# Two constants of RMSNorm in one tile, and the tiles behind them 32 bytes lower in SBUF

## The chip, the cores and the metric

The kernel runs on one core of a Trainium2 chip. The metric is the device time of one execution in microseconds (us); lower is better. Three runs of the kernel before were timed, and one further execution was profiled.

## What is computed

The reference chains three blocks on 3072 tokens of width 512:

```
# 1. chunked attention: 4 x 8 heads, 768 positions, head width 64; chunks of 32 queries see
#    16 positions to the left, 8 to the right, and 8 memory slots
a = exp(s - max(s)); a = a / (sum(a) + 1e-9); x = a @ v          # s = q k^T / 8
# 2. first MoE block, d_ff 1536
xn = x / sqrt(mean(x * x) + 1e-6) * rms_g
y = (silu(xn @ w_gate) * (xn @ w_val)) @ w_out
# 3. second MoE block, d_ff 2048
h = y @ w_in
g = where(h >= 1, h, where(h <= -1, 0, (h + 1)**2 / 4))
out = g @ w_out2
```

## The kernel before

**Stages.** Tokens are handled in 6 tiles of 512 (`TT`). The opening (0 to 36 us of the profile) runs the attention of the first 256-token pairs by an order written out by hand (`ORDER`): `s` is the scores, `m` and `e` their softmax, `a` and `A` a transpose, `v` the product with the values, `n`, `q`, `k` and `p` the normalization, `x` and `X` a transpose of the result. Then the first MoE block takes four of the six tiles one by one (36 to 496 us); the rest of the attention, the conversion of the weights from 64-bit words, and the making of weight sums for later stages run in the slots between its matmuls (`slot`, `att_slot`, `conv_w`, `conv_step`). The last two tiles of the first MoE block go together as a pair (496 to 690 us), and then the second MoE block runs in three pairs of tiles, both with seven products in place of eight.

**Matmuls.** Each product of two float32 matrices is made of three matmuls on a high and a low part (`mm3`, lines 546 to 548; lines 854 to 856 and 990 to 992 in the later stages). In the first MoE block the weights are the stationary operand, from the tile `wall`, and the streamed operand is `xh`, `xl` (the normalized input) or `hh`, `hl` (the hidden values), tiles of 512 float32 columns, 2048 bytes a partition.

**The constants.** `rms_g` is loaded twice by SP, once spread over all partitions as rows (`g_b`, line 629), and once as 4 columns, one for each block of 128 features (`g_t`, line 630). `nhalf` is two columns of -0.5, set by VectorE at the start (line 589). `part_p` (line 498) raises the mean square to the power -0.5 on GpSimd with `nhalf` as the exponent, twelve times, once a pair. From the third pair on `part_X` (line 535) scales by the columns of `g_t` on ScalarE; the first two pairs are multiplied by `g_b` (lines 509 and 651).

**Memory.** Tiles are taken from pools, in the order of the code, each a multiple of 32 bytes a partition. On the left side lie `const` (`half`), `wpool` (`wall`, 147456 bytes), and then the pools of the first MoE block: `const1` with `ident` (512 bytes), `g_b` (2048), `nhalf` (8) and `g_t` (16), then `small`, `wst`, `tmp`, `xs`, `hp`, `sp` and `sums`. The pool `att` of the attention lies on the right side, up to the end of the memory; its tiles `k0`, `k1`, `q`, the rows, `aT` and `e` are 2048 bytes, the two `v` buffers 2080. The last of the left pools ends where `att` begins. When the single tiles are done, `p1` takes the place of `xs` and what follows it; when the first MoE block is done, the pool `m2` begins where `ident` was.

```python
    ident = const1.tile([P, P], F32, name="ident")
    g_b = const1.tile([P, DM], F32, name="g_b")
    nhalf = const1.tile([P, 2], F32, name="nhalf")
    g_t = const1.tile([P, KK], F32, name="g_t")
```

**What sets the order.** In the opening the order on every engine is that of the code. In the first of the four tiles (to about 150 us) the order on TensorE and SP is that of the code, and a planner orders the other engines by its own costs. After that every engine follows the code again. Waits between engines and for transfers are derived from which tiles an instruction reads and writes.

Of the kernel before, what the change touches and what calls it, by code (L numbers as in the profile page):

```python
# [8 lines left out]
F32 = mybir.dt.float32  # L9
# [7 lines left out]
P = 128  # L17
# [21 lines left out]
def tile_stream_attention_moe_moe2(  # L39
# [14 lines left out]
    KK = DM // P  # L54
# [15 lines left out]
    const1 = pool1("const1", 1)  # L70
# [13 lines left out]
    wall = wpool.tile([P, 36, 2, 512], F32R, name="wall")  # L84
    ident = const1.tile([P, P], F32, name="ident")
    g_b = const1.tile([P, DM], F32, name="g_b")
    nhalf = const1.tile([P, 2], F32, name="nhalf")
    g_t = const1.tile([P, KK], F32, name="g_t")


    busy = sums_.tile([P, TT], F32, tag="s34", name="busy").bitcast(BF16)[:, :FILL]
# [1048 lines left out]
```

## Time and profile before

| | us |
|---|---|
| median of 3 runs | 1179.17 |
| lowest and highest run | 1174.78, 1180.15 |
| span of the profiled execution, first to last instruction | 1172.9 |
| matmuls busy in that span | 1151.0 |
| VectorE, ScalarE, GpSimd busy | 741.2, 517.6, 108.0 |

The profiled execution's own time is known by its span. The timed runs also hold what lies before the first and after the last instruction. Busy times are those of the profile; matmuls overlap, so that their durations don't add up to time.

### The profile page before, as it was taken

What the parts mean: (1) busy time and instruction counts of PE and PEld (TensorE: products, weight loads), DVE (VectorE), ACT (ScalarE), POOL (GpSimd) and SP (SyncE); (2) the same over time, 40 slices, a digit from 0 to 9 for tenths busy, and PEclk for the clock granted to TensorE, in tenths of its full rate; (3) what the DMA queues carried; (4) which work ended last, traced back from release to release, by engine and by line L of the source; (5) the groups of instructions that cost most, each with busy time, mean ns of one, the idle gap of its engine ahead of it and who ended that gap; (6) DMA issues with size and microseconds to landing.
All of it is one profiled execution on the core that took longest, in us unless ns stands there. A gap on an engine that the chain in (4) does not pass through costs nothing.

```text
span 1172.9 us, 19949 instructions
## 1 busy us (share of the span) xinstructions
PE 1151.0 (98%) x7993; PEld 936.4 (80%) x7993; DVE 741.2 (63%) x1280; ACT 517.6 (44%) x910; POOL 108.0 (9%) x175
## 2 busy tenths in 40 slices
PE   6899999999999999999999999999999999999998
PEld 4677878887778778878888888888888888888887
DVE  5888865566465655877677576665376662576620
ACT  4766756556665664433333343333143341343310
POOL 2200012212122122201111000000000000000000
PEclk9899999999999999999999999999999999999999
DMA  8566467788767666598898775757466576555364
GB/s 307 177 221 208 153 223 275 282 290 294 276 206 239 223 199 225 199 383 311 305 361 309 283 279 189 261 187 267 158 222 260 195 259 203 191 190 197 135 202 157
DMA packets 98589, 278.60 MB, mean 238 GB/s; under 512 B 10560, under 2 KB 22848, under 8 KB 92096
## 3 DMA queue, kind: packets, MB, share of 16 engines
q1 hardware_dynamic: 79936, 218.59, 52.5%
q0 software_dynamic: 15104, 52.44, 12.3%
q10 hardware_dynamic: 3456, 6.29, 1.4%
q8 instruction: 63, 1.03, 0.3%
q14 instruction: 30, 0.25, 0.1%
HBM read 209.13 MB, written 68.16 MB: 236 GB/s over the span
## 4 chain that ended last, share of the span: by engine, by line
PE 86%; DMA 6%; DVE 4%; ACT 2%; issue 1%; POOL 0%; SPq 0%; ACTq 0%; DVEq 0%; POOLq 0%
PE ps_y L991 7%; PE ps_y L992 7%; PE ps_y L990 7%; PE ps_g L546 6%; PE ps_g L547 6%; PE ps_g L548 6%; PE ps_b L855 5%; PE ps_b L854 5%; PE ps_b L856 5%; PE ps_y L546 5%; PE ps_y L547 5%; PE ps_y L548 5%; PE ps_g L854 4%; PE ps_g L855 4%; PE ps_g L856 4%; DMA w<-in_w_dram 3%
## 5 line engine op out<-in xcount | busy, mean ns | idle before, releaser
L546 PE MATMUL ps_g<-xh,wall 128*128 128x512 f32 x384 | 156.3, 407 | 0.0
L547 PE MATMUL ps_g<-xl,wall 128*128 128x512 f32 x384 | 150.9, 393 | 0.0
L548 PE MATMUL ps_g<-xh,wall 128*128 128x512 f32 x384 | 150.4, 392 | 0.0
L914 ACT ACTIVATE t<-t,half 128x512 f32<-128x512 f32 x96 | 69.0, 720 | 131.2 <-DVE t L913 131.2
L991 PE MATMUL ps_y<-wo,wall 128*128 128x512 f32 x324 | 126.0, 389 | 0.0
L990 PE MATMUL ps_y<-wo,wall 128*128 128x512 f32 x324 | 126.0, 389 | 0.0
L992 PE MATMUL ps_y<-wo,wall 128*128 128x512 f32 x324 | 126.0, 389 | 0.0
L854 PE MATMUL ps_b<-wall 128*128 128x512 f32 x288 | 112.0, 389 | 0.0
L855 PE MATMUL ps_b<-wall 128*128 128x512 f32 x288 | 112.0, 389 | 0.0
L856 PE MATMUL ps_b<-wall 128*128 128x512 f32 x288 | 112.0, 389 | 0.0
L928 DVE TENSOR_TENSOR t<-t,ps_g 128x512 f32<-128x512 f32 x24 | 16.5, 688 | 113.5 <-PE ps_g L856 107.9
L548 PEld LDWEIGHTS ps_g<-xh,wall 128*128 128x128 f32 x384 | 72.6, 189 | 16.1
L854 PE MATMUL ps_g<-wall 128*128 128x512 f32 x216 | 84.2, 390 | 1.1 <-DMA wall<-w1p_d 1.0
L546 PEld LDWEIGHTS ps_g<-xh,wall 128*128 128x128 f32 x384 | 72.6, 189 | 15.8
L855 PE MATMUL ps_g<-wall 128*128 128x512 f32 x216 | 84.1, 389 | 0.0
L856 PE MATMUL ps_g<-wall 128*128 128x512 f32 x216 | 84.0, 389 | 0.0
L547 PEld LDWEIGHTS ps_g<-xl,wall 128*128 128x128 f32 x384 | 72.8, 190 | 13.5
L546 PE MATMUL ps_y<-hh,wall 128*128 128x512 f32 x192 | 77.6, 404 | 0.0
L547 PE MATMUL ps_y<-hl,wall 128*128 128x512 f32 x192 | 75.2, 392 | 0.1
L548 PE MATMUL ps_y<-hh,wall 128*128 128x512 f32 x192 | 74.9, 390 | 0.0
L990 PEld LDWEIGHTS ps_y<-wo,wall 128*128 128x128 f32 x324 | 60.8, 188 | 12.7
L991 PEld LDWEIGHTS ps_y<-wo,wall 128*128 128x128 f32 x324 | 60.8, 188 | 12.6
(157 smaller groups left out, 2240.4 us busy)
## 6 DMA issues: line engine op xcount, KB each, us to landing
wo<-w2o_d SPq DMA_DIRECT2D x100, 512.0 KB, 4.8
wall<-w2p_d SPq DMA_DIRECT2D x24, 1792.0 KB, 7.3
wall<-w1p_d SPq DMA_DIRECT2D x12, 1792.0 KB, 8.6
w<-in_w_dram SPq DMA_DIRECT2D x36, 512.0 KB, 3.9
w<-in_w_dram POOLq DMA_DIRECT2D x32, 512.0 KB, 5.5
k_in<-in_k_dram SPq DMA_DIRECT2D x48, 256.0 KB, 4.6
wo<-w1o_d SPq DMA_DIRECT2D x24, 512.0 KB, 7.9
v_in<-in_v_dram SPq DMA_DIRECT2D x40, 260.0 KB, 4.3
```

Of the source, the lines that this page charges most:

```text
L546: nc.tensor.matmul(ps, wh, xh, start=start, stop=False)
L547: nc.tensor.matmul(ps, wh, xl, start=False, stop=False)
L548: nc.tensor.matmul(ps, wl, xh, start=False, stop=stop)
L854: nc.tensor.matmul(bank, wh, xh, start=st, stop=False, skip_group_check=True)
L855: nc.tensor.matmul(bank, wh, xl, start=False, stop=False, skip_group_check=True)
L856: nc.tensor.matmul(bank, wl, xh, start=False, stop=kk == 1, skip_group_check=True)
L914: nc.scalar.activation(s, s, AF.Square, scale=0.5, bias=half)
L928: tt(out=u2, in0=a, in1=b2, op=ALU.add)
L990: nc.tensor.matmul(ps_y[m], hi[:, sl], wh, start=b == 0, stop=False)
L991: nc.tensor.matmul(ps_y[m], hi[:, sl], wl, start=False, stop=False)
L992: nc.tensor.matmul(ps_y[m], lo[:, sl], wh, start=False, stop=b == F2 - 1)
```

## The change

The tiles `nhalf` and `g_t` become one tile `facts` of 6 columns. Its first 4 columns take the place of `g_t`, the last 2 that of `nhalf`. The names stay, as views of the tile. The code that writes and reads them is unchanged.

```diff
     ident = const1.tile([P, P], F32, name="ident")
     g_b = const1.tile([P, DM], F32, name="g_b")
-    nhalf = const1.tile([P, 2], F32, name="nhalf")
-    g_t = const1.tile([P, KK], F32, name="g_t")
+    facts = const1.tile([P, KK + 2], F32, name="facts")
+    g_t, nhalf = facts[:, :KK], facts[:, KK:]
```

The tiles of the left pools behind `const1` begin 32 bytes lower in each partition: those of `small`, `wst`, `tmp`, `xs`, `hp`, `sp` and `sums`, and later those of `p1`. `wall`, `ident`, `g_b`, the pool `att` and the pool `m2` stay where they are.

## Rows read from the trace of the kernel before

**Rows 1.** The page's first part: busy us (share of the span) and instructions by engine

```profile
PE 1151.0 (98%) x7993; PEld 936.4 (80%) x7993; DVE 741.2 (63%) x1280; ACT 517.6 (44%) x910; POOL 108.0 (9%) x175
```

**Rows 2.** Busy time by stretch: from:to, length, engines, granted clock, DMA share, GB/s

```profile
0.00:36.00 36.00, 23.70 (x651) 16.11 (x652) 21.45 (x45) 17.26 (x41) 13.01 (x18) 0.91 0.88 301
36.00:496.00 460.00, 455.70 (x4387) 365.81 (x4386) 315.73 (x596) 278.36 (x522) 71.04 (x117) 0.99 0.66 229
690.00:1172.90 482.90, 478.88 (x2113) 396.18 (x2111) 269.96 (x431) 153.89 (x236) 0.00 (x0) 1.00 0.58 208
...
36.00:100.00 64.00, 61.34 (x444) 49.05 (x442) 58.30 (x108) 44.85 (x85) 3.89 (x4) 0.94 0.55 188
```

**Rows 3.** Groups of instructions by line: count, busy us, mean ns, idle before

```profile
L546 PE MATMUL ps_g<-xh,wall 128*128 128x512 f32 x384 | 156.3, 407 | 0.0
...
L546 PE MATMUL ps_y<-hh,wall 128*128 128x512 f32 x192 | 77.6, 404 | 0.0
```

**Rows 4.** Timeline of TensorE in the first MoE block: start, duration, instruction

```profile
470.24 0.39 PE L546 MATMUL ps_g<-xh,wall 128*128 128x512 f32 x1
...
471.60 0.39 PE L546 MATMUL ps_g<-xh,wall 128*128 128x512 f32 x1
```

**Rows 5.** Timeline of TensorE in the paired tiles

```profile
559.62 0.39 PE L854 MATMUL ps_b<-wall 128*128 128x512 f32 x1
...
560.98 0.39 PE L854 MATMUL ps_b<-wall 128*128 128x512 f32 x1
```

**Rows 6.** Timeline of the opening, what touches the constants and follows them

```profile
1.20 0.06 DVE L589 MEMSET nhalf<- 128x2 f32 x1
...
14.28 0.43 SPq L630 DMA_DIRECT2D g_t<-in_rms_g_dram  x1
...
20.51 3.16 POOL L651 TENSOR_TENSOR x_nat<-x_nat,g_b 128x256 f32<-128x256 f32 x4 [19.20 <-ACT sq L479]
...
23.64 1.16 POOL L498 TENSOR_TENSOR rs<-ss,nhalf 128x2 f32<-128x2 f32 x1
...
24.83 0.72 ACT L655 ACTIVATE x_nat<-x_nat,rs 128x512 f32<-128x512 f32 x1 [0.64 <-POOL rs L498]
...
25.61 0.66 PE L519 MATMUL ps_s<-ident,x_nat 128*128 128x128 f32 x4 [0.70 <-ACT x_nat L655]
```

**Rows 7.** The tile g_t: its load, and from issue to landing

```profile
L630 SPq DMA_DIRECT2D g_t<-in_rms_g_dram x1: 433/433/433, 14.3 to 14.3; - x1
...
DMA to landing us min/median/max: 5.5/5.5/5.5
```

**Rows 8.** The tiles v_in, then k_in: from issue to landing

```profile
DMA to landing us min/median/max: 2.6/4.4/7.5
...
DMA to landing us min/median/max: 2.7/4.6/8.7
```

**Rows 9.** Lines 463 and 498: duration ns min/median/max, first and last start

```profile
L463 DVE RECIPROCAL rd<-rd x24: 195/203/206, 16.6 to 436.1; 128x8 f32<-128x8 f32 x24
...
L498 POOLq EVENT_SEMAPHORE x1: 17/17/17, 77.2 to 77.2; - x1
```

**Rows 10.** Lines 439 and 393, matmuls of the attention, the same columns

```profile
L439 PE MATMUL ps_a<-v_in,aT x1392: 213/217/263, 16.0 to 435.7; 64*32 64x65 f32 x199
...
L393 PE MATMUL ps_a<-k_in,q_in x1344: 212/216/241, 5.8 to 422.3; 64*32 64x64 f32 x192
```

**Rows 11.** Waits of TensorE: us in total, times, longest us

```profile
PE ps_a L393 <- DMA q_in<-in_q_dram: 2.0, 2, 1.5
...
PE ps_s L393 <- DMA q_in<-in_q_dram: 1.2, 1, 1.2
PE ps_g L854 <- DMA wall<-w1p_d: 1.0, 1, 1.0
```

**Rows 12.** Timeline of the opening: matmuls that fill time

```profile
14.96 1.07 PE L95 MATMUL ps_a<-busy 128*128 128x352 bf16 x6
...
8.62 0.77 PE L95 MATMUL ps_s<-busy 128*128 128x352 bf16 x4
```

## The prediction

> **What bounds the kernel now.** I read the page's totals first, then busy time by stretch, then the groups of instructions, then the waits, and last the few instructions that touch the two constants.
>
> The totals put TensorE at 1151.0 of 1172.9 us [rows 1]: whatever the change does must reach TensorE to count. By stretch [rows 2], the opening 36 us hold 23.70 us of matmuls, the first MoE with attention beside it (36 to 496 us) 455.70 of 460, the last stretch shown 478.88 of 482.90. Outside the opening there are 4.3 + 4.0 us of idle TensorE in those two stretches, and the only wide place is 36 to 100 us (61.34 of 64), where VectorE is busy for 58.30 of 64 us with the conversion of the weights. The matmuls that read a moved tile as their streamed operand are the three lines 546 to 548 with xh, xl, hh or hl [rows 3]: 3 x (384 + 192) = 1728 of them. Their duration is a pipelined latency; what one costs is the distance from start to start. In 470.24 to 471.60 us six pass, 1.36 / 6 = 0.227 us each [rows 4]. In 559.62 to 560.98 us, with operands in the weights' tile, which doesn't move, six pass in the same 1.36 us [rows 5].
>
> The profiled execution has a span of 1172.9 us; the runs have a median of 1179.17, 6.3 us more, which I take as what lies around the span and leave as it is.
>
> **The change, part by part.** *What is added or removed as work: nothing.* The memset of two columns, the 2 KB load, the twelve powers and the scalings are the same instructions. The sum therefore has only waits and addresses in it.
>
> *The shared tile.* If order is kept by tile and not by column, two waits are new. First, the load on SP waits for the memset: that ran at 1.20 us, the load is issued at 14.28 us [rows 6], slack 13 us, cost 0. Behind it on SP stand the loads of v and of the weights; they keep their place. Second, the first power (L498, GpSimd) waits for the load. It lands 5.5 us after its issue [rows 7], at 19.8 us, and the power starts at 23.64 us because GpSimd is in its four multiplications by g_b from 20.51 us on [rows 6]: slack 3.9 us, cost 0. Were that cover gone, the scaling on ScalarE at 24.83 us and then the transposes at 25.61 us would be late by as much, 1 us for 1 us. Of the 48 loads of k the slowest took 8.7 us [rows 8]; with that the constants would land at 22.98 us, still before 23.64. A wait written as an instruction of its own takes 17 ns [rows 9]; only the two powers of the opening have TensorE behind them, so 0.03 us. I take 0.0. The later readers of the constants come after this load by tens of us; all of them are covered.
>
> *The 32 bytes.* Tiles take multiples of 32 bytes: 8 and 16 bytes took two such steps, 24 bytes take one. The pools start on a multiple of 64; `half` takes 32, so the weights, `ident` and `g_b` begin 32 past a multiple of 64, and today everything behind `g_t` does too, since all other tiles there are multiples of 64, or come in pairs of 32. After the change those tiles begin on a multiple of 64, while the weights stay at 32 past. The pool of the second MoE starts where `ident` did and doesn't move; the boundaries of the two pools never coincide (they differ by half of 512 bytes), so a shift of 32 makes no later tile lie over another earlier one, and the waits for reuse stay as they are. What is left is whether an access at 64n + 32 costs other than one at 64n. The trace has three controls, because a few tiles of before lie at both.
>
> VectorE: `rd` has two buffers 32 bytes apart, one at each position. All 24 reciprocals take 195 to 206 ns [rows 9]. The bound is that spread, 11 ns. Where VectorE nearly fills the time (36 to 100 us) it has 108 instructions [rows 2]: 108 x 11 ns = 1.2 us to either side. Elsewhere TensorE has work queued; 0 there. I take 0.
>
> TensorE: a chunk of v is 65 columns, 260 bytes, so successive chunks begin at every multiple of 4 bytes within a 64-byte line; chunks of k are 256 bytes and begin all at one position. The medians are 217 and 216 ns, the least 213 and 212 [rows 10], and the one column more accounts for that. I take 0; as a bound, 1 ns on each of 1728 matmuls is 1.7 us to either side. This control has 64 columns and a float32 stream rather than 512 columns, so it is near, not the same.
>
> Transfers: of the two v buffers of the attention pool one is 2080 bytes behind the other, so at 64n, the other at 64n + 32; all k buffers are at 64n + 32. The medians to landing are 4.4 us for 260 KB and 4.6 us for 256 KB [rows 8]. I take 0; the bound is 0.2 us a transfer. TensorE itself waits for a transfer in four places shown [rows 11], 4.2 us in all: 4 x 0.2 = 0.8 us to either side.
>
> The sum: 1172.9 + 0.0 in the profile, 1179.2 in runs, bounds 1.2 + 1.7 + 0.8 = 3.7 us to either side. For order I add the 4.3 us of idle TensorE in 36 to 496 us: there ScalarE, VectorE and GpSimd are ordered by a planner that sees one tile where it saw two; the most a changed order is likely to do is to lose or give back something of that size. That makes 1171 to 1187 at the outside.
>
> *A rule against the row.* The trace's distance of 227 ns for 512 columns is longer than its own bfloat16 filling matmuls suggest: six take 1.07 us and four 0.77 [rows 12], so 0.15 us for 352 columns, and 218 ns for 512. Nine ns of each large matmul are unexplained by columns. The Trainium skill ("TensorE: Matmul & The Clock Gate", Back-to-back issue gap) gives N/2.4 + 2.5 ns for a matmul at the full clock, 215.8 ns here, so by it too about 11 ns are extra; by that page 1728 x 11 = 19 us would be to be won if the place of the rows were the reason. The Trainium skill ("SBUF — State Buffer", Specifications) puts SBUF's lines at 16 bytes; by that a shift of 32 changes nothing in how a row falls on lines, the extra has another cause, and the sum stays at 0. The controls above agree with the second.
>
> **The rivals.**
>
> *TensorE gets faster.* A row of 2048 bytes at 64n + 32 touches one line of 64 more than a row at 64n; if that is the 9 ns, 1728 x 9 = 15.6 us go: 1164. For it: the extra is there, and every large matmul of before streams from 64n + 32. Against it: the filling matmuls also stream from 64n + 32 and show no extra, and the chunks of v show none. Chance 0.07.
>
> *TensorE gets slower.* After the change the streamed row is at 64n and the weights are at 64n + 32; today both have the same place. If weight load and stream get in each other's way when out of step, and a matmul pays as much again as it does now, 9 ns, the time is 1179.2 + 15.6 = 1195. It decides from 5.9 us / 1728 = 3.4 ns a matmul on. For it: the weight load overlaps the stream in every matmul. Against it: the chunks of v meet their weights at all positions, with 217 ns as median. Chance 0.05.
>
> *The shared tile stalls the opening.* The power waits for a late load. It needs a landing 23.64 - 14.28 = 9.4 us after the issue to cost anything and 9.4 + 5.9 = 15.3 us to cost 0.5%; the slowest load in [rows 8] took 8.7. It stays inside the forecast.
>
> *The change moves nothing* (the space is rounded otherwise, or a planner lays tiles out anew): then the time is 1179 too, and only the addresses would tell.
>
> **How the numbers follow.** A measurement of this kernel can tell about 0.5%, 5.9 us, from no change; its three runs lie 5.4 us apart. No change holds 0.76: the sum is 0 and its bounds of 3.7 us are inside. Faster 0.13: the first rival 0.07, and 0.06 for gains at their bounds together with a better order of the planner. Slower 0.11: the second rival 0.05, and 0.06 for the bounds on the other side, order included. The forecast is 1179 us, the range 1171.5 to 1186.5: the sum with its bounds and the term for the order. It leaves out both rivals on TensorE, 0.12, and a little beyond the bounds.
>
> **What would show it.** In the profile after: the start-to-start distance of lines 546 to 548 stays 0.227 us (a rival if 0.218 or 0.236); reciprocals at 195 to 206 ns and v loads at 4.4 us; the first power starts at about 23.6 us with GpSimd busy before it, and no wait for g_t's load in front of it; TensorE busy for about 455.7 us between 36 and 496. I would be wrong if that distance moved by more than 3.4 ns, if the idle TensorE time of 36 to 100 us doubled, or if an order of instructions on VectorE or ScalarE came out different and cost a wait for weights.

## The result: slower by 0.7%

The changed kernel takes 1185.49 us (median of 4 runs, 1183.39 to 1187.11), the kernel before 1176.97 us on the same chips (4 runs, 1173.36 to 1180.15). The ratio is 1.0072 with an interval of 1.0055 to 1.009: some 8.5 us are lost, outside noise. The forecast was no change, 1171.5 to 1186.5 us; the time lies just inside that range, but the change is real and the forecast was wrong. That it lies inside is luck: the terms that made the range wide (reciprocals, transfers, order) showed no effect, and the kernel before came out 2.2 us below the 1179.17 us that the forecast started from; 1179.17 + 8.5 would lie outside.

The page's totals after, the same line as in [rows 1]:

```profile
PE 1159.8 (98%) x7993; PEld 936.1 (79%) x7993; DVE 741.2 (63%) x1280; ACT 518.1 (44%) x910; POOL 107.8 (9%) x175
```

VectorE, ScalarE and GpSimd are where they were, with the same counts of instructions. TensorE is busy 8.8 us longer with the same 7993 matmuls, and its share stays at 98%: a stream of matmuls that have become slower looks as full as before. The shared tile is innocent in the profile. In the timeline of the opening after (start, duration, engine, instruction) the load is issued at 14.39 us, and the first power follows the four multiplications at once, as in [rows 6]:

```profile
14.39 0.43 SPq L630 DMA_DIRECT2D facts<-in_rms_g_dram  x1
...
20.66 3.17 POOL L651 TENSOR_TENSOR x_nat<-x_nat,g_b 128x256 f32<-128x256 f32 x4 [19.35 <-ACT sq L479]
...
23.79 1.16 POOL L498 TENSOR_TENSOR rs<-ss,facts 128x2 f32<-128x2 f32 x1
```

The controls on VectorE and on transfers stand too: reciprocals still take 203 ns, and the loads of v land after 4.2 us (4.4 in [rows 8]). What moved is the matmul. The timeline of TensorE after, in the same stretch as [rows 4]:

```profile
469.61 0.40 PE L547 MATMUL ps_g<-xl,wall 128*128 128x512 f32 x1
...
471.94 0.40 PE L548 MATMUL ps_y<-hh,wall 128*128 128x512 f32 x1
```

Ten matmuls pass between these two starts, 2.33 / 10 = 0.233 us each, where it was 0.227. The duration shows it as well. Line 547 by its three uses, the inputs and outputs of the single tiles and the outputs of the paired tiles (duration ns min/median/max, first and last start). Before:

```profile
L547 PE MATMUL ps_g<-xl,wall x384: 387/389/628, 39.3 to 490.9; 128*128 128x512 f32 x192
L547 PE MATMUL ps_y<-hl,wall x192: 387/389/497, 51.4 to 496.7; 128*128 128x512 f32 x192
...
L547 PE MATMUL ps_y<-wall,wo x96: 389/389/496, 516.4 to 678.3; 128*128 128x512 f32 x96
```

After:

```profile
L547 PE MATMUL ps_g<-xl,wall x384: 390/396/404, 38.8 to 495.5; 128*128 128x512 f32 x192
L547 PE MATMUL ps_y<-hl,wall x192: 389/396/461, 51.0 to 501.2; 128*128 128x512 f32 x192
...
L547 PE MATMUL ps_y<-wall,wo x96: 392/396/498, 520.9 to 688.3; 128*128 128x512 f32 x96
```

The third row is the surprise: these are the outputs of the paired tiles. Their streamed row lies in `wall`, which did not move. Their weights (`wo`, in the pool `p1`) did. And the products of the later stages, and the outputs of the second MoE block, keep their 389 ns (lines 854 and 990 after):

```profile
L854 PE MATMUL ps_b<-wall x288: 388/389/398, 504.4 to 1123.7; 128*128 128x512 f32 x144
...
L990 PE MATMUL ps_y<-wo,wall x324: 388/389/398, 708.2 to 1167.2; 128*128 128x512 f32 x162
```

So exactly those matmuls became slower of whose two operands one moved and the other stayed. Taken over all neighbouring starts less than 300 ns apart in the two traces, the mean distance (start to start) goes from 228.5 to 233.2 ns in the first MoE block (1561 and 1571 pairs) and from 226.9 to 233.2 in the paired outputs (284 and 282 pairs); the other stages stay at 226.7. With 1728 and 288 matmuls that is 1728 x 4.7 + 288 x 6.3 = 9.9 us, against 8.5 measured.

### The profile page after: what moved, and what is told of

Read it like the earlier page. It is cut to its first block, busy times and chain, and to the rows that moved or that the text cites. A ratio compares the mean times of both kernels' runs of the same rounds, so it can differ in the third digit from the quotient of the medians.

```text
span 1183.0 us, 19949 instructions
## 1 busy us (share of the span) xinstructions
PE 1159.8 (98%) x7993; PEld 936.1 (79%) x7993; DVE 741.2 (63%) x1280; ACT 518.1 (44%) x910; POOL 107.8 (9%) x175
## 4 chain that ended last, share of the span: by engine, by line
PE 89%; DMA 5%; DVE 3%; ACT 2%; issue 1%; SPq 0%; POOL 0%; ACTq 0%; DVEq 0%; POOLq 0%
PE ps_y L992 7%; PE ps_y L991 7%; PE ps_y L990 7%; PE ps_g L546 7%; PE ps_g L548 6%; PE ps_g L547 6%; PE ps_b L856 5%; PE ps_b L854 5%; PE ps_b L855 5%; PE ps_y L546 5%; PE ps_y L547 5%; PE ps_y L548 5%; PE ps_g L854 4%; PE ps_g L856 4%; PE ps_g L855 4%; DMA w<-in_w_dram 2%
```

## The experiments

Three theories were put on record. *Step*: a large matmul costs more when its streamed row and its weights lie at different places; operands at equal places, counted modulo a period that the experiments had to find, are called in step below. *Place*: a row or weights at a multiple of 64 bytes cost more by themselves. *Wait*: sharing the tile adds a wait or changes an order.

**Shared tile, old places** (`e1_gap`).

```diff
     facts = const1.tile([P, KK + 2], F32, name="facts")
+    gap = const1.tile([P, 2], F32, name="gap")
...
+    nc.vector.memset(gap, 0.5)
```

> The changed kernel with an unused tile of 8 bytes behind the shared one (and one memset of it), so that every later tile lies where it lay before. Theory step (a large matmul costs more when its streamed row and its weights lie at different places within 64 bytes): the distance of lines 546 to 548 is back at 0.227 us and the time at that of before, 1177 us. Theory place (a row at a multiple of 64 costs more by itself): the same, 1177. Theory wait (sharing the tile adds a wait or changes the planner's order): it stays near 1185 us.

Measured: 1178.6 us, ratio 1.0002 (0.9992 to 1.0013). In the trace the distance is 228.4 ns in the first MoE block and 226.9 in the paired outputs, those of before. Sharing the tile costs nothing; *wait* falls, and the whole loss is in the 32 bytes. The line that is 547 in the other kernels (`e1_gap`):

```profile
L548 PE MATMUL ps_g<-xl,wall x384: 387/389/402, 40.7 to 491.7; 128*128 128x512 f32 x192
```

**Everything at a multiple of 64** (`e2_all0`).

```diff
-    half = const.tile([P, 1], F32, name="half")
...
     wall = wpool.tile([P, 36, 2, 512], F32R, name="wall")
+    hold = wpool.tile([P, 16], F32, name="hold")
+    half, g_t, nhalf = hold[:, :1], hold[:, 1:KK + 1], hold[:, KK + 1:KK + 3]
...
-    nhalf = const1.tile([P, 2], F32, name="nhalf")
-    g_t = const1.tile([P, KK], F32, name="g_t")
```

> Weights and all other left tiles begin at a multiple of 64 bytes (half, g_t and nhalf share a tile of 64 bytes behind the weights). Streamed rows and weights are in step again, but at 64n, not at 64n + 32. Theory step: 0.227 us everywhere, 1177 us. Theory place: all 4680 large matmuls cost some 6 ns more than before, 0.233 us in every stage, about 1204 us. Should the period be 128 bytes instead of 64, the second MoE block alone shows 0.233 us where weights or rows come from its own pool, which lies 64 bytes out of step here.

Measured: 1180.48 us, ratio 1.0015 (1.0006 to 1.0025). The first MoE block is at 228.3 ns, as before. *Place* falls: 1204 us was its forecast. The small loss that is left sits in the second MoE block, whose pool lies 64 bytes off here. The three lines of its outputs, where rows come from that pool and weights from `wall` (`e2_all0`, lines one up from the original):

```profile
L989 PE MATMUL ps_y<-wo,wall x324: 392/394/398, 700.1 to 1162.7; 128*128 128x512 f32 x162
...
L990 PE MATMUL ps_y<-wo,wall x324: 388/388/397, 700.3 to 1162.9; 128*128 128x512 f32 x162
...
L991 PE MATMUL ps_y<-wo,wall x324: 388/392/398, 700.6 to 1163.1; 128*128 128x512 f32 x162
```

Their mean distance is 229.3 ns: 64 bytes cost something, but less than 32. So the period isn't 64 bytes.

**The weights alone moved** (`e3_wall0`).

```diff
-    half = const.tile([P, 1], F32, name="half")
...
     wall = wpool.tile([P, 36, 2, 512], F32R, name="wall")
+    half = wpool.tile([P, 1], F32, name="half")
```

> The weights' tile alone moves 32 bytes down, to a multiple of 64 (half lies behind it); all other tiles are where they were before, and nhalf and g_t are two tiles. Theory step: 0.233 us in the first MoE block, in the outputs of the paired tiles and in the outputs of the second MoE block whose other operand is the weights' tile (972 matmuls), 0.227 us in the products, where both operands lie in the weights' tile; 1177 + 8 + 2 + 6 = 1193 us. Theory place: the products (1512 matmuls) cost 6 ns more as well, about 1203 us.

Measured: 1190.48 us, ratio 1.0099 (1.0085 to 1.0112), nearer to *step* (1193) than to *place* (1203). The trace parts them. Outputs of the second MoE block with weights from `wall`, with weights from the block's own pool, and products with both operands in `wall` (`e3_wall0`):

```profile
L991 PE MATMUL ps_y<-wo,wall x324: 393/394/397, 706.7 to 1173.1; 128*128 128x512 f32 x162
L991 PE MATMUL ps_y<-wo,h x60: 387/389/389, 836.8 to 1184.0; 128*128 128x512 f32 x60
...
L854 PE MATMUL ps_b<-wall x288: 389/389/389, 505.6 to 1128.2; 128*128 128x512 f32 x144
```

The first and the second row are the same line of code, with the same rows. Only the place of the weights differs.

**The matmul by itself** (`m1_grid`). One line for each pair of places, for weights `w` and streamed row `x`, both of the type float32r in which the large matmuls of the kernel run (the profile writes f32):

```python
    N = 60
...
    for i in range(N): nc.tensor.matmul(ps[1], w(32, i), x(0), start=i == 0, stop=i == N - 1)
```

> Attention and both MoE blocks are left out and the output is zeros; 36 groups of 60 large matmuls (128x128 weights, 512 columns, float32r) run one after the other, with weights and streamed row beginning 0, 16, 32, 48, 64 or 96 bytes behind a multiple of 128. Nothing else runs beside them. Theory step: the distance depends on the difference of the two places alone, 227 ns for 0 and 64, 233 ns for 32; 16 and 48 are not known from the kernels. Theory place: it depends on each place, not on the difference. A third theory, that the extra comes from other engines' accesses to the same memory and the places only shift what they meet: all groups at one distance, 227 ns or less.

The timeline of TensorE in `m1_grid`: each row is one group; start to start of two groups, over 60, is the cost of a matmul of the first. Lines 85 to 87 have the weights at 32 bytes and the row at 0, 16 and 32; lines 97, 99 and 101 have the weights at 64 and the row at 0, 32 and 64:

```profile
178.61 14.16 PE L85 MATMUL ps<-xt,wt 128*128 128x512 f32 x60
192.61 14.16 PE L86 MATMUL ps<-xt,wt 128*128 128x512 f32 x60
206.61 13.79 PE L87 MATMUL ps<-xt,wt 128*128 128x512 f32 x60
220.24 14.06 PE L88 MATMUL ps<-xt,wt 128*128 128x512 f32 x60
...
344.53 14.15 PE L97 MATMUL ps<-xt,wt 128*128 128x512 f32 x60
358.52 14.24 PE L98 MATMUL ps<-xt,wt 128*128 128x512 f32 x60
372.60 14.16 PE L99 MATMUL ps<-xt,wt 128*128 128x512 f32 x60
386.60 13.77 PE L100 MATMUL ps<-xt,wt 128*128 128x512 f32 x60
400.20 13.80 PE L101 MATMUL ps<-xt,wt 128*128 128x512 f32 x60
413.84 14.17 PE L102 MATMUL ps<-xt,wt 128*128 128x512 f32 x60
```

Out of step (lines 85, 97, 99): 14.0 / 60 = 233.3 ns. In step (87, 101): 13.63 / 60 = 227.2 ns with the first matmuls of a group still settling. No other engine and nearly no transfer runs beside them, so the theory of other engines falls as well. At places that are a multiple of 32 the difference decides, as *step* says, but one of its prices was missed: for a difference of 64 it wanted 227 ns, and a row 64 bytes above its weights costs 228.9, a row 64 bytes below them (line 97) 233.3. At 16 and 48 the difference doesn't decide: equal places at 16 give (123.36 - 109.49) / 60 = 231 ns by the same timeline, and a row at 32 with weights at 16 gives 226.7.

**The whole kernel in step, 128 bytes apart** (`e5_step`) **and only the first block in step** (`e6_moe1`). Both take the changed kernel and the edit of `e3_wall0`; `e5_step` also has

```diff
     m2["pool"] = ctx.enter_context(tc.tile_pool(name="m2", bufs=1, reuse_waits="tile"))
+    m2["pool"].tile([P, 24], F32, name="gap")
```

> The changed kernel (one shared tile, all tiles behind it 32 bytes lower) with the weights' tile 32 bytes lower too (half lies behind it) and the pool of the second MoE block 96 bytes higher, so that all three are a multiple of 128 bytes apart. Theory step: 0.227 us in every stage and the time of before, 1178 us here, ratio 1.000 to 1.002. Any theory in which the 32 bytes or the shared tile cost by themselves: ratio 1.007, as the changed kernel.

> As e5_step, but the pool of the second MoE block stays where it was in the kernels before and after, which is now 32 bytes out of step with the weights' tile. Theory step: the first MoE block is at 0.227 us, and the 972 matmuls of the second block's outputs that mix both places are at 0.233 us: 972 x 6.5 ns = 6.3 us, ratio 1.005. The loss moves from the first block to the second. The 180 outputs whose stationary operand comes from the second block's own pool stay at 0.227.

Measured: `e5_step` 1184.76 us, ratio 1.0057 (1.0044 to 1.007); `e6_moe1` 1185.38 us, ratio 1.006 (1.0039 to 1.0081). The second came as expected: the loss moved from the first block, now at 228.2 ns, to the outputs of the second, now at 233.4 (`e6_moe1`):

```profile
L991 PE MATMUL ps_y<-wo,wall x324: 393/394/397, 701.5 to 1168.0; 128*128 128x512 f32 x162
```

The first was a miss, and the trace says where. Line 547 in the first MoE block is back at 389, and the outputs of the second block (line 991), at a difference of 128 bytes, are not (`e5_step`):

```profile
L547 PE MATMUL ps_g<-xl,wall x384: 387/389/628, 39.7 to 492.0; 128*128 128x512 f32 x192
...
L991 PE MATMUL ps_y<-wo,wall x324: 387/394/404, 700.7 to 1166.5; 128*128 128x512 f32 x162
```

Their mean distance is 233.1 ns. Neither 64 nor 128 is the period. In the kernel before, rows and weights of the first block lie 256 bytes apart modulo 512 and pass at the in-step distance, so 256 can be.

**Batches, and other shapes** (`m2_detail`).

> Attention and both MoE blocks are left out and the output is zeros. First part: 20 large matmuls at a time, each batch behind eight small matmuls of the attention's kind, for 11 differences between the place of the streamed row and that of the weights (0 to 256 bytes), at two places of the weights; it asks how quickly a batch settles, and whether the period is 128 bytes (then 128 and 256 are as 0, and 160 is as 32). Second part, 60 at a time at differences of 0, 32 and 64 bytes: 256 columns instead of 512, weights of 32 columns instead of 128, and bfloat16. Theory collision (the load of the next weights and the stream get in each other's way, once a matmul): 256 columns lose as much as 512, some 6.6 ns a matmul at 32 bytes; with weights of 32 columns the loss is smaller or gone. Theory stream (the loss is spread over the columns): 256 columns lose half, 3.3 ns, and weights of 32 columns lose the full 6.6. For bfloat16 neither says: 216 ns if it has none of it.

Differences of 128 and 160 bytes (weights at 32) end at 232.8 and 234.0 ns in the last eight of each batch, 256 bytes at 226.7, as 0 does: for places at multiples of 32 the period is 256 bytes. With the weights at 48 the rows differ, as in `m1_grid`: 230.9 ns at a difference of 0, 231.1 at 256, and 226.7 at 160. A batch in step needs some ten matmuls behind the small ones until it is at 227; in between the distances swing between 224 and 236. This is why the first block of the kernel before, which attention interrupts, has a mean of 228.5 and not 226.7: its first ten distances behind a piece of attention have means of 228 to 234 ns by their place in the row, the later ones together 226.7. The other shapes, by the timeline of `m2_detail`: lines 149 to 151 have 256 columns at differences of 0, 32 and 64 bytes, lines 156 and 157 are bfloat16 at 32 and 64:

```profile
571.65 7.36 PE L149 MATMUL ps<-xt,wt 128*128 128x256 f32 x60
578.85 7.24 PE L150 MATMUL ps<-xt,wt 128*128 128x256 f32 x60
585.92 7.23 PE L151 MATMUL ps<-xt,wt 128*128 128x256 f32 x60
...
647.71 13.11 PE L156 MATMUL ps<-xb,wb 128*128 128x512 bf16 x60
660.66 13.11 PE L157 MATMUL ps<-xb,wb 128*128 128x512 bf16 x60
```

256 columns cost 7.20 / 60 = 120 ns in step and 7.07 / 60 = 118 out of step: less, where *collision* wanted 6.6 ns more and *stream* 3.3. Both fall as they stand. Weights of 32 columns cost 231.7, 233.3 and 231.7 ns at 0, 32 and 64: a smaller loss, as *collision* wanted, but a matmul in step is then slower too. bfloat16 has (660.66 - 647.71) / 60 = 215.8 ns at 32 bytes, and the settled starts (the last 40 distances of a group) give the same 215.8 at 0 and 64: no step at these three.

**Full step** (`e7_step256`). `e5_step` with the gap at `[P, 56]`, 224 bytes, so that the three areas are a multiple of 256 apart.

> As e5_step, with the pool of the second MoE block 224 bytes higher instead of 96, so that weights, first MoE tiles and second MoE tiles are a multiple of 256 bytes apart (in e5_step the second block was 128 apart). Theory step with a period of 256 bytes: 0.227 us in every stage, ratio 1.000 to 1.002 to the kernel before, with the shared tile and the 32 bytes both still in. If a period of 128 had been right and e5_step was slow for another reason: 1.006 again.

Measured: 1177.22 us, ratio 1.0001 (0.9989 to 1.0013). The shared tile is in, the 32 bytes are in, and the time is that of before. The same two rows as for `e5_step`:

```profile
L547 PE MATMUL ps_g<-xl,wall x384: 387/389/496, 38.1 to 490.9; 128*128 128x512 f32 x192
...
L991 PE MATMUL ps_y<-wo,wall x324: 389/389/395, 700.4 to 1159.6; 128*128 128x512 f32 x162
```

**All differences, and widths** (`m3_cols`).

> Attention and both MoE blocks are left out and the output is zeros. Groups of 60 large float32r matmuls. First the differences of 32 to 256 bytes between streamed row and weights, with the weights at 0 and at 32 bytes behind a multiple of 256: by the step theory with a period of 256 the distance depends on the difference alone, 227 ns at 256, 229 at 64, 233 or more at 32, 96, 128, 160, 192 and 224. Then 192 to 480 columns, and weights of 96 and 64 columns, each at differences of 0, 32 and 224 bytes. Theory collision: the loss at 32 and 224 bytes is 6.6 ns a matmul for any number of columns. Theory stream: it grows with the columns. The 256 columns of m2_detail spoke against both, with a gain of 2.3 ns; if that goes on at other widths, neither holds and the inner cause stays open.

The timeline of `m3_cols`, weights at 32 bytes, lines 80 to 87 with differences of 32, 64, 96, 128, 160, 192, 224 and 256 bytes:

```profile
124.30 14.16 PE L80 MATMUL ps<-xt,wt 128*128 128x512 f32 x60
138.30 13.91 PE L81 MATMUL ps<-xt,wt 128*128 128x512 f32 x60
152.05 14.17 PE L82 MATMUL ps<-xt,wt 128*128 128x512 f32 x60
166.06 14.16 PE L83 MATMUL ps<-xt,wt 128*128 128x512 f32 x60
180.06 14.21 PE L84 MATMUL ps<-xt,wt 128*128 128x512 f32 x60
194.11 14.16 PE L85 MATMUL ps<-xt,wt 128*128 128x512 f32 x60
208.11 14.16 PE L86 MATMUL ps<-xt,wt 128*128 128x512 f32 x60
222.11 13.79 PE L87 MATMUL ps<-xt,wt 128*128 128x512 f32 x60
235.73 13.16 PE L88 MATMUL ps<-xt,wt 128*128 128x480 f32 x60
```

Over 60: 233.3, 229.2, 233.5, 233.3, 234.2, 233.3, 233.3 and, at 256, 227.0. With the weights at 0 the settled distances agree within 0.1 ns at each difference. The kernels fit the table without exception:

| kernel | places of `wall`, first MoE tiles, second pool | first MoE, ns | paired outputs, ns | second outputs, ns | ratio |
|---|---|---|---|---|---|
| before | 32, 32, 32 | 228.5 | 226.9 | 226.7 | 1 |
| after | 32, 0, 32 | 233.2 | 233.2 | 226.7 | 1.0072 |
| `e1_gap` | 32, 32, 32 | 228.4 | 226.9 | 226.7 | 1.0002 |
| `e2_all0` | 0, 0, 64 | 228.3 | 227.0 | 229.3 | 1.0015 |
| `e3_wall0` | 0, 32, 32 | 233.2 | 233.1 | 233.4 | 1.0099 |
| `e5_step` | 0, 0, 128 | 228.2 | 226.8 | 233.1 | 1.0057 |
| `e6_moe1` | 0, 0, 32 | 228.2 | 226.8 | 233.4 | 1.006 |
| `e7_step256` | 0, 0, 0 | 228.3 | 227.1 | 226.7 | 1.0001 |

(Places are bytes modulo 256 from the first tile of the left side, added up from the sizes of the tiles; only their differences are used. Distances are means of neighbouring starts under 300 ns apart; the second outputs are those with weights in `wall`.) With other widths there is no plain law: settled, 480 columns cost 216.7 ns in step and 220.0 out of it; 448 cost 202.7, and 206.7 or 204.5 at differences of 32 and 224; 416 cost 188.3, and 186.7 or 190.0; and 384, 320 and 192 cost the same at all three. Nor is there one for narrower weights: 96 columns of weights cost 230.0 ns in step, and 233.3 or 228.9 at 32 and 224, 64 columns 229.9, and 230.8 or 231.7.

## Why the prediction was wrong

**The shared tile** was read rightly: both new waits are covered, and `e1_gap` puts their price at 0.0002 of the time, within its interval of 0.

**The step that failed is the control for TensorE** in "The 32 bytes". It took the chunks of v, 65 columns at many places, as a bound of 1 ns for large matmuls, "near, not the same". It was not near: they are float32 matmuls of 65 columns on a quarter-width array, and even at float32r the step vanishes at 192, 320 and 384 columns and turns round at 256. A control has to share the property in question; here that was 512 columns streamed back to back against a weight load. The trace of before held no such matmul out of step, and the honest bound was the unexplained 9 ns, to either side. The same holds for the filling matmuls, bfloat16, which were held against an extra: bfloat16 has none at the three differences measured.

**What happened was on the list, at 0.05.** "TensorE gets slower" named the condition, streamed row and weights out of step, and the place where it shows. The reason that it gave, weight load and stream in each other's way, isn't shown: the 256 columns speak against it. Its price of 9 ns was mis-sized: it is 4.7 ns in the first MoE block, because there the kernel before already loses 1.8 ns to settling, and 6.3 ns in the paired outputs. It also counted 1728 matmuls where 2016 have one moved operand: the working looked for moved rows and passed over the 288 paired outputs, whose weights moved. "TensorE gets faster" falls with `e2_all0`: rows at 64n alone gain nothing, and 226.7 ns is the least that any of the places gave.

**The rules.** The Trainium skill ("SBUF — State Buffer", Specifications) puts lines at 16 bytes, from which a shift of 32 looked free; the measured 6.6 ns at 32 bytes decide otherwise for float32r matmuls of this width. The N/2.4 + 2.5 ns of the Trainium skill ("TensorE: Matmul & The Clock Gate", Back-to-back issue gap), there the gap of an isolated matmul, which the prediction left out, agrees with the distance of bfloat16 matmuls in `m2_detail`, 215.8 ns, and not with that of float32r, 226.7 at best.

**Smaller steps.** Reciprocals, transfers and waits for reuse were right. The sum of distances, 9.9 us, is more than the 8.5 measured. In the profiles, which are single executions, the first block, from the first start of line 546 to that of line 854, grows by 4.7 us and not by 8.1. Part of the difference is the clock of the execution before: from 87.5 to 90.9 us, behind 2.66 us in which TensorE waited for ScalarE, its granted clock was 0.50 (the 1.2 GHz level), and large matmuls started 0.43 us apart there. `e1_gap`, with the old places and no such stretch in the block, takes 457.7 us for it, against 463.2 after, so the growth is 5.5 us. The rest lies where TensorE would have waited: distances of over 300 ns between or behind large matmuls add up to 45.8 us in `e1_gap` and 43.3 after. The stage of the pair grows by 5.6 us, from 201.0 to 206.6, of which its matmuls explain 1.8. TensorE waits longer for transfers there after (2.0 us for `w1p_d`, 1.0 before [rows 11], and 0.8 for `w1o_d`, none before), and behind the first of these waits the granted clock falls. The timeline after, and busy time with the granted clock (third number from the end) in that stretch after and in the one of before:

```profile
525.61 0.47 PE L854 MATMUL ps_g<-wall 128*128 128x512 f32 x1 [1.96 <-DMA wall<-w1p_d]
...
526.66 0.63 PE L854 MATMUL ps_g<-wall 128*128 128x512 f32 x1
...
529.79 0.40 PE L856 MATMUL ps_g<-wall 128*128 128x512 f32 x1
```

```profile
526.00:529.40 3.40, 3.40 (x10) 2.61 (x9) 0.00 (x0) 1.15 (x2) 0.00 (x0) 0.51 0.90 383
...
87.50:90.90 3.40, 3.40 (x11) 2.62 (x10) 2.67 (x6) 3.40 (x9) 0.00 (x0) 0.50 0.58 188
```

From the first to the last of the twelve matmuls behind that wait it takes 529.79 - 525.61 = 4.18 us; before, behind a wait of 1.0 us at full clock, 2.61. So the 5.6 us are 1.8 from the matmuls out of step, 1.8 from longer waits, 1.6 from the clock, and 0.4 unexplained. `e1_gap` waits 1.6 and 0.7 us at the same two places and keeps the full clock, so the clock and most of the waits belong to these executions and not to the change.

What happens inside TensorE stays open: the loss depends on both operands' places, with 128 columns of weights it was clear at 448, 480 and 512 streamed columns and full at 512 alone, and neither a collision once a matmul nor a loss per column fits.

None of the versions beats the kernel before. A difference of 112 bytes also gave 226.7 ns in `m2_detail`, settling within two matmuls, and so did some other pairs with a tile at an odd multiple of 16 bytes; none was tried in the kernel.

## What to carry to other kernels

When a kernel is bound by float32r matmuls of 512 columns, the distance between the addresses of streamed tiles and weight tiles, modulo 256 bytes, is a tuning parameter worth 3% of each matmul; a small tile added or removed anywhere below shifts it. Look at start-to-start distance, not at busy share, which stayed at 98%. And ask of a control in the trace whether it shares the width, the type and the rate of what it stands for; if not, it bounds nothing.

## What the runs showed of the hardware

- float32r, 128x128 weights, 512 columns, full granted clock (2.4 GHz level): 226.7 ns when row and weights are equal modulo 256 bytes, both at a multiple of 32; 228.9 with the row 64 bytes above the weights; 233.3 to 234.4 at the other multiples of 32. The sign counts: +64 is cheap, -64 (the same as +192) is not. With both at 16 or both at 48 it was 231.1 and 230.0.
- bfloat16 at 512 columns: 215.8 ns at 0, 32 and 64 bytes.
- float32r at 256 columns: 120.0 ns in step, 117.7 at 32 bytes; at 384, 320 and 192 columns no difference.
- After eight small matmuls (`m2_detail`), or a piece of attention (the kernel before), a stream of large ones in step takes about ten matmuls to settle at 226.7 ns.
- At a granted clock of 0.5 (the 1.2 GHz level) the same matmuls start 427 ns apart, against 227 to 234 at the full one (after, 526.0 to 529.4 us).
